# One new order of work for a two-part transformer layer, with w_phi first, Wk ahead, and eight filling products for fourteen

## The chip, the cores and the metric

The kernel runs on one core of one Trainium2 chip. The metric is the time of one execution in microseconds (us), the median of several runs; lower is better. A core has a matrix engine (TensorE, PE in the views, with its weight loads as PEld), VectorE (DVE), ScalarE (ACT), GpSimd (POOL) and SyncE (SP). Each engine works through its own queue strictly in the order of the program; semaphores hold an instruction until what it needs is there. Transfers between memory and the core are issued from the queue of an engine, here SP's or ACT's.

## What is computed

The input has 2048 rows of 640 values, in bfloat16. An attention with feature maps and a gated block follow each other, each behind a layer norm and with its input added:

```python
def _A_ref(x, wqkv, w_phi, wo):          # 32 heads of 20
    q, k, v = ...                        # x @ wqkv, split by head
    pq = einsum("bhsd,hdf->bhsf", q, w_phi)
    pk = einsum("bhsd,hdf->bhsf", k, w_phi)
    phi_q = concat([softmax(pq), softmax(-pq)])
    phi_k = concat([softmax(pk), softmax(-pk)])
    kv = einsum("bhsf,bhsd->bhfd", phi_k, v)
    z  = einsum("bhsf->bhf", phi_k)
    num = einsum("bhqf,bhfd->bhqd", phi_q, kv)
    den = einsum("bhqf,bhf->bhq", phi_q, z)[..., None] + 1e-6
    return (num / den) @ wo

h  = x + _A_ref(layernorm(x), wqkv, w_phi, wo)
n  = layernorm(h)
h2 = h + ((n @ w_gate) * (n @ w_up)) @ w_down
```

## The kernel before

The rows are cut into 16 tiles of 128. The work is a graph of some 1,030 named operations, built in `build_graph`. Each has a name of a kind and a tile. The kinds that the text needs, in the order in which a tile meets them:

- `x0`, `x1`, ... load tiles of x; `w5` loads w_phi; `wk0` to `wk4` and `wv0` to `wv4` load 128 rows each of Wk and Wv; `wqt0` to `wqt4` load Wq transposed. All are transfers.
- `warm0`, ... multiply zeros (lines 367 and 372). They stand in TensorE's queue while it has nothing else; eight come first (L367) and `NFILL` more after (L372).
- `WT0` to `WT4` transpose Wk on TensorE (L392), `WTe0`, ... copy the result out (L251), `Ph0` to `Ph2` spread w_phi into a block matrix Phi on GpSimd (L380), and `F1_0` to `F1_4` multiply Wk by Phi (L411), so that one product gives the argument of the feature map. `Fe1_0`, ... copy that out. `F0_0` to `F0_4` do the same for Wq, and read all five `wqt`.
- `L1s`, `L1a` take the statistics of a tile on VectorE (L428, L429, L431), `L1l`, `L1e` its inverse deviation by a logarithm and an exponential on ScalarE (L436, L439), `L1n` a shift, and `xn` scales the tile (L453 on VectorE, L451 on ScalarE). `xt` transposes the scaled tile: tiles 0 and 1 on TensorE (L462, copied out by `xte`), the others by a transposing transfer from SP's queue (L471).
- `V`, `K`, `Q` are the three projections of a tile (L482); for tiles 0 and 1 each is cut into five pieces (`K0_0` to `K0_4`). `Ve` copies V out (L251). For K, `Kx` are two exponentials (L494), `Ks` their sums (L498), `Kr` and `Ke` a logarithm and an exponential of these (L501, L503), `Kn` the scaling on GpSimd (L518), and `KV` adds the tile to the sum over rows (L526). The Q kinds `Qx`, `Qs`, `Qr`, `Qb`, `Qe`, `Qn` do the like (L551 to L570), and `qT` transposes by a transfer.
- `KVe0` and `KVe1` take the sum out (L533). Then, tile by tile, `N` gives numerator and denominator (L588), `dd`, `rd`, `o` divide, `oT` transposes by a transfer, `O` multiplies by wo (L625), `h` adds x (L631), `hc` and `hT` center and transpose, `L2q`, `L2v`, `L2r` give the second norm's factor.
- The gated block takes the rows in five groups (tiles 0 and 1, 2 to 5, 6 to 9, 10 to 13, 14 and 15, numbered 0 to 4). `U0_1_0` is the product with w_gate for group 0 and columns block 1, `U0_1_1` that with w_up (L668); `g` copies the gate out on ScalarE (L673), `u` multiplies on VectorE (L676). `D` is the product with w_down for a tile (L687), `y` adds (L699) and `w` stores.

What decides the order is the dictionary `PLAN`, read from a long text at the head of the kernel. An entry has the operation's name, a key, the number of an alternative engine and the numbers of the buffer slots, for example:

```python
x1:0.78:1 ekz:0.78 x0:0.78 zero:0.91 id0:1.014 warm0:1.127
```

`arrange` sorts all operations by key, and every engine gets its own in that order. Keys are compared only, so they may be times or ranks. The slots name, among others, the eight banks of PSUM ("psum") in which TensorE leaves its products. An operation that takes a slot waits for the last reader of the one that had it before: so a projection waits for the exponentials or the copy of an earlier one. The waits on semaphores are worked out in `emit` from these orders.

At the head the queues stand as follows before. SP: x0, x3, w5, wk0, wk4, wk1, wk2, x4 (two tiles), wv1, wv0, wv2, wv3, x2, wv4, x6. ACT: x1, wk3. TensorE: 18 products on zeros, WT3, three more, WT0, xt1, WT4, WT1, the last on zeros, F1_0, F1_3, WT2, xt0, F1_1, F1_4, F1_2, then pieces of K0, K1, V1, V0. VectorE: L1s1, L1s0, L1a1, L1s3, L1a0, xn1, L1a3, WTe0, xn0, WTe4, xn3, WTe2, xte0.

Of the kernel before, what the change touches and what calls it, by code (L numbers as in the profile page):

```python
# [69 lines left out]
Fe0_0:26.481 L1s13:26.984 xn9:27.065:1:0 F0_4:27.378::4 K4:27.697::0 Kr5:27.88 Fe0_4:27.895:1 xt9:28.018 Ve6:28.026::6 mk0:28.408 mk1:28.572 Kr2:28.61  # L70
L1s11:28.635 Ke2:28.901 Fe0_2:29.047 KV0:29.053::4,5 Kn2:29.235 wd1:29.328 KV1:29.386 L1s10:29.422 Kx4_0:29.631::2 K7:29.719::2 L1s14:30.209 Kx4_1:30.215
F0_3:31.075::6 L1a14:31.119 L1a10:31.228 Kx7_0:31.275::0 xn8:31.337::1 V7:31.394::0 smz:31.548 Fe0_3:31.859 L1a11:31.867 xt8:31.975 Ks4:31.976::1 Kx7_1:32.443
KV2:32.75 Ke5:33.027 KV3:33.083 L1l10:33.173 wg1:33.285 L1s15:33.369 F0_1:33.416::6 L1e10:33.499 K6:33.735::2 L1n11:33.779 Fe0_1:33.933 Kn5:34.003
# [164 lines left out]
def build_graph():  # L238
# [131 lines left out]
    wm_b = Buf("pwarm", "psum")  # L370
    for k in range(8, 8 + NFILL):
        G.op("pe", "warm%d" % k, lambda e: e.matmul(pb(wm_b)[:, 0:256], lhsT=T["zero"][:, 0:P], rhs=T["zero"][:, :],  # L372
# [556 lines left out]
```

## Time and profile before

| what | value |
|---|---|
| time, median of 3 runs | 271.48 us (271.42 to 271.83) |
| profiled execution, first to last instruction | 270.1 us |
| granted TensorE clock, mean | 1.000 |
| TensorE busy | 264.2 us, 98% |
| VectorE busy | 160.0 us, 59% |
| ScalarE busy | 124.0 us, 46% |
| GpSimd busy | 71.3 us, 26% |

The profile is of one execution. It covers the span from the first to the last instruction; the timed runs hold 1.4 us more, which lie around the span. In a row of the timeline the columns are start, duration from the first start to the last end, engine, line, operation, what is written and read, and the count; in brackets stands the idle time of the engine before it and what ended that. The end of a product is modelled and holds its way through the array, so a run of products is read by its starts. A row of busy time by stretches has, for the stretch, its length, then the busy time of PE, PEld, DVE, ACT and POOL with the number of instructions, the granted clock, the share of the DMA engines and the GB/s. A row of the chain that ended last has start, length and what ran.

### The profile page before, as it was taken

What the parts mean: (1) busy time and instruction counts of PE and PEld (TensorE: products, weight loads), DVE (VectorE), ACT (ScalarE), POOL (GpSimd) and SP (SyncE); (2) the same over time, 40 slices, a digit from 0 to 9 for tenths busy, and PEclk for the clock granted to TensorE, in tenths of its full rate; (3) what the DMA queues carried; (4) which work ended last, traced back from release to release, by engine and by line L of the source; (5) the groups of instructions that cost most, each with busy time, mean ns of one, the idle gap of its engine ahead of it and who ended that gap; (6) DMA issues with size and microseconds to landing.
All of it is one profiled execution on the core that took longest, in us unless ns stands there. A gap on an engine that the chain in (4) does not pass through costs nothing.

```text
span 270.1 us, 5186 instructions
## 1 busy us (share of the span) xinstructions
PE 264.2 (98%) x2092; PEld 177.9 (66%) x2105; DVE 160.0 (59%) x294; ACT 124.0 (46%) x316; POOL 71.3 (26%) x89
## 2 busy tenths in 40 slices
...
GB/s 200 318 168 136 249 222 129 302 183 245 204 106 143 163 126 149 140 123 64 171 93 2 0 0 36 57 106 1 73 12 2 0 0 51 49 1 0 27 49 61
DMA packets 71752, 28.09 MB, mean 104 GB/s; under 512 B 59056, under 2 KB 71728, under 8 KB 71728
## 3 DMA queue, kind: packets, MB, share of 16 engines
...
## 4 chain that ended last, share of the span: by engine, by line
PE 90%; DMA 5%; DVE 2%; ACT 1%; issue 1%; SPq 1%; DVEq 0%
PE ps L668 36%; PE ps L482 24%; PE ps L687 19%; PE ps L625 6%; DMA scratch<-ph 2%; PE ps L526 2%; PE ps L588 2%; DMA Wp<-o 2%; DMA x_all<-in_A_x_dram 1%; PE ps L411 1%; SPq L653 1%; DVE st L428 0%; ACT Wp L251 0%; DVE st L429 0%; DVE ev L676 0%
## 5 line engine op out<-in xcount | busy, mean ns | idle before, releaser
L668 PE MATMUL ps<-xnT,Wgu 128*128 128x512 bf16 (+1 forms) x587 | 106.0, 335 | 0.7
L668 PEld LDWEIGHTS ps<-xnT,Wgu 128*128 128x128 bf16 x600 | 58.3, 98 | 43.4
L673 ACT ACTIVATE gt<-ps 128x512 bf16<-128x512 f32 (+1 forms) x60 | 29.7, 509 | 100.9 <-PE ps L668 62.9
L482 PE MATMUL ps<-Wp,xnT 128*128 128x320 bf16 (+1 forms) x480 | 68.6, 298 | 0.0
L482 PEld LDWEIGHTS ps<-Wp,xnT 128*128 128x128 bf16 x480 | 45.5, 97 | 17.2 <-issue 0.2
L676 DVE TENSOR_TENSOR ev<-ps,gt 128x512 bf16<-128x512 f32 (+1 forms) x60 | 33.6, 579 | 36.5 <-PE ps L668 27.8
L687 PE MATMUL ps<-Wd,ev 128*128 128x320 bf16 (+2 forms) x396 | 53.9, 295 | 0.0
L687 PEld LDWEIGHTS ps<-Wd,ev 128*128 128x128 bf16 x396 | 38.1, 98 | 15.3 <-DVE ev L676 0.2
L699 DVE SCALAR_TENSOR_TENSOR Wp<-ps,rs,x_all 128x640 bf16<-128x640 f32 (+3 forms) x18 | 14.6, 810 | 49.3 <-PE ps L687 49.1
L518 POOL TENSOR_TENSOR ek<-ek,SR 128x1280 bf16<-128x1280 bf16 x16 | 37.5, 2358 | 5.2 <-ACT SR L503 5.1
L551 ACT ACTIVATE ph<-ps 128x600 bf16<-128x600 f32 x32 | 21.4, 680 | 8.0 <-PE ps L482 6.9
L556 DVE TENSOR_REDUCE S<-ph 128x66 f32<-128x1320 bf16 x16 | 23.9, 1516 | 1.8 <-ACT ph L553 1.8
L625 PE MATMUL ps<-Wo,Wp 128*128 128x320 bf16 x160 | 23.9, 299 | 0.2
L498 DVE TENSOR_REDUCE SR<-ek 128x64 f32<-128x1280 bf16 x16 | 23.3, 1468 | 1.0 <-ACT ek L494 1.0
L570 POOL TENSOR_TENSOR ph<-ph,RQ 128x660 bf16<-128x660 bf16 x16 | 20.7, 1308 | 8.9 <-ACT RQ L566 8.9
L646 POOL TENSOR_SCALAR ln<-mv 128x1 f32<-128x1 f32 x12 | 2.3, 191 | 75.7 <-ACT ek L642 75.1
L494 ACT ACTIVATE ek<-ps 128x640 bf16<-128x640 f32 x32 | 21.2, 719 | 2.2 <-PE ps L482 1.5
L625 PEld LDWEIGHTS ps<-Wo,Wp 128*128 128x128 bf16 x160 | 15.3, 98 | 6.4 <-DMA Wp<-o 0.4
L631 DVE SCALAR_TENSOR_TENSOR x_all<-ps,x_all 128x640 bf16<-128x640 f32 x16 | 13.1, 821 | 6.4 <-PE ps L625 6.4
L615 DVE TENSOR_TENSOR o<-ps,sm 128x660 bf16<-128x660 f32 x16 | 13.4, 840 | 0.9 <-ACT sm L608 0.6
L642 ACT ACTIVATE ek<-x_all,mv 128x640 bf16<-128x640 bf16 x16 | 13.1, 821 | 0.0
L251 ACT ACTIVATE ev<-ps 128x640 bf16<-128x640 f32 x16 | 11.2, 704 | 1.1 <-PE ps L482 1.1
...
## 6 DMA issues: line engine op xcount, KB each, us to landing
out_dram<-Wp SPq DMA_DIRECT2D x15, 160.0 KB, 1.8
...
Wp<-in_A_wqkv_dram SPq DMA_DIRECT2D x5, 160.0 KB, 4.7
ev<-in_A_wqkv_dram SPq DMA_DIRECT2D x4, 160.0 KB, 4.2
x_all<-in_A_x_dram SPq DMA_DIRECT2D x3, 160.0 KB, 3.2
```

The source lines that it names most:

```text
L482: ins = e.matmul(pb(b, hb)[:, 0:n1 - n0], lhsT=T["xnT"][:, NC - 1 - c, P * t:P * (t + 1)], rhs=T["Wp"][:, POS[kind], c, n0:n1], start=(c = ...
L494: G.op("act", "%sx%d_%d" % (nm, t, s), lambda e, s=s, b=b, ek=ek: e.activation(out=T["ek"][:, ek.slots[0], 0:2 * D].rearrange("p (b h s f) ...
L498: G.op("dve", "%ss%d" % (nm, t), lambda e, ek=ek, sr=sr: e.tensor_reduce(out=T["SR"][:, sr.slots[0], 0, :], in_=T["ek"][:, ek.slots[0], 0: ...
L518: G.op("pool", "Kn%d" % t, lambda e, eng, ek=ek, sr=sr: e.tensor_tensor(out=T["ek"][:, ek.slots[0], 0:2 * D].rearrange("p (h f) -> p h f", ...
L551: e.activation(out=v[:, 0:10].rearrange("p (b g) j f -> p b g j f", b=2), in_=pp(b, 0, 300).rearrange("p b (g j f) -> p b g j f", j=3, f=D ...
L556: G.op("dve", "Qs%d" % t, lambda e, t=t, ph=ph: e.tensor_reduce(out=T["S"][:, t, 0:66].rearrange("p (g k) -> p g k", k=6), in_=pv(ph).rear ...
L570: return e.tensor_tensor(out=v, in0=v, in1=T["RQ"][:, rq.slots[0], 1, 0:33].rearrange("p (g j) -> p g j", j=3).unsqueeze(3).to_broadcast([ ...
L625: ins = e.matmul(pb(b, hb)[:, 0:320], lhsT=T["oT"][:, oT.slots[0], c, :], rhs=T["Wo"][:, c, 320 * hb:320 * (hb + 1)], start=(c == 0), stop ...
L668: ins = e.matmul(pb(b)[:, 0:n], lhsT=T["Wgu"][:, gu, c, P * ft:P * (ft + 1)], rhs=T["xnT"][:, NC - 1 - c, o0:o0 + n], start=(c == 0), stop ...
L673: G.op("act", "g%d_%d" % (bi, ft), lambda e, pg=pg, gt=gt, n=n: e.activation(out=T["gt"][:, gt.slots[0], 0:n], in_=pb(pg)[:, 0:n], func=AF ...
L676: o_ = G.op("dve", "u%d_%d" % (bi, ft), lambda e, pu=pu, gt=gt, hh=hh, ft=ft, n=n: e.tensor_tensor(out=T["hh"][:, hh.slots[0], ft, 0:n], i ...
L687: ins = e.matmul(pb(b, hb)[:, 0:w], lhsT=T["hh"][:, hh.slots[0], ft, P * tt:P * (tt + 1)], rhs=T["Wd"][:, ft, c0 + w * hb:c0 + w * (hb + 1 ...
```

## The change

`PLAN` is replaced as a whole, with ranks from 0 to 1023 as keys, and `NFILL` goes from 14 to 8. No operation other than six products on zeros is added or dropped, and no formula changes. What moves, by engine:

- SP's queue begins w5, x1, x3, wk0, wk3, wk2, wk1, wv1, wv0, wv2, x2, wv3, x4, x6, wv4, xt3, wqt4, xt2, wqt2, xt4, xt5, wqt3, wqt1, xt6, wqt0. ACT's queue begins x0, wk4, and later issues x8, x10, wu2 and wd3.
- TensorE: 13 products on zeros, WT4, three more, xt0, F1_4, WT0, WT3, xt1, WT2, WT1, F1_0, F1_3, V0_0, V0_1, F1_2, V0_2, F1_1, V0_3, V1_0, K0_0. The projections after these come as K3, V3, K2, V4, K5, V5, V2, V6 (before: K3, V3, K5, V5, K2, V2, V4).
- VectorE begins L1s0, L1a0, L1s1, xn0, L1a1, L1s3, xn1, L1a3, WTe0, WTe3, xte1, WTe1, Fe1_0. Six copies of V (Ve0, Ve1, Ve8, Ve11, Ve13, Ve14) go from ScalarE to VectorE; xn5 and xn6 go to ScalarE, where xn9 was.
- ScalarE from xn2 on: xn2, Kx1_0, L1l4, Kx1_1, L1e4, Kx0_0, Kx0_1, xn5, L1l6, Kx3_0, L1e6, x10, Kx3_1, Kr0, Ve3, xn6, Kx2_0, Kx2_1, Kr1, Ke0, Ke1, Ve4, L1l8, Kx5_0, Kr3, Ve5, L1e8, Ke3, Ve2, Kx5_1.
- The second half has more of group 0 and group 1 before the last numerators, and D5, D4, D3 and D0 behind each other. The last products are D14, D13, D11, D12, D10, D15_1, D15_2 (before: D14, D11, D13, D12, D10, D15_1, D15_2).

The diff, cut to the lines that the text speaks of:

```diff
-NFILL = 14
+NFILL = 8
...
-x1:0.78:1 ekz:0.78 x0:0.78 zero:0.91 id0:1.014 warm0:1.127 id1:1.252 x3:1.26:1 wk3:1.26:1 warm1:1.345 va1:1.496 warm2:1.564 w5:1.74:1 warm3:1.782 warm4:2.001
-warm5:2.219 wk0:2.22:1 eps:2.326 gl0:2.357 warm6:2.437 gla:2.518 warm7:2.656 wk4:2.7:1 glb:2.822 warm8:2.874::0 warm9:3.093 wk1:3.18 warm10:3.311 warm11:3.529
-wk2:3.66:1 L1s1:3.725 warm12:3.748 warm13:3.966 x4:4.14 warm14:4.185 warm15:4.403 L1s0:4.512 wv1:4.62 warm16:4.621 warm17:4.84 wv0:5.1:1 L1a1:5.299 L1s3:5.408
-WT3:5.446::1 L1l1:5.532 wv2:5.58:1 Ph2:5.775 L1e1:5.858 warm18:5.902 warm19:6.011 wv3:6.06 WTe3:6.1:1 warm20:6.12 L1a0:6.195 xn1:6.304::0 Ph1:6.369 x2:6.54
-WT0:6.546::2 L1l0:6.685 Ph0:6.761 L1a3:6.834 xt1:6.971::3 wv4:7.02:1 WTe0:7.023:1 L1l3:7.067 L1e0:7.249 WT4:7.25::4 L1e3:7.393 xte1:7.486 xn0:7.487::1 x6:7.5
-L1n3:7.673 WT1:7.746::5 phz:7.897 WTe4:8.017:1 warm21:8.025 F1_0:8.134::6 WTe1:8.223:1 xn3:8.425::2 F1_3:8.453::0 WT2:8.772::2 Fe1_0:8.808:1 xt0:9.051::3
-xt3:9.063 WTe2:9.249:1 F1_1:9.33::4 Fe1_3:9.392 F1_4:9.649::6 xte0:9.657:1 Fe1_1:9.976 L1s4:10.065 F1_2:10.153::0 x8:10.373 K0_0:10.472::2 Fe1_2:10.67:1
-K0_1:10.743 L1s5:10.852 wqt4:10.853 K1_0:11.014::4 Fe1_4:11.254:1 K1_1:11.285 K1_2:11.556 L1a4:11.639 L1a5:11.762 V1_0:11.827::0 L1l4:11.995 K1_3:12.098
-wqt1:12.163 L1s2:12.225 L1e4:12.321 V0_0:12.369::6 K1_4:12.64 V1_1:12.911 L1n5:13.012:1 Kx1_0:13.11::0 V0_1:13.182 xn5:13.296::3 V0_2:13.453 Kx1_1:13.694
...
-L1l6:18.929 xt4:19.174 L1e6:19.255 Ks3:19.347::1 Ve3:19.348::2 L1n7:19.535 L1n6:19.759 Kx0_0:19.932::2 V5:19.96::0 rqz:19.983 wqt3:20.484 Kx0_1:20.516
...
-L1e8:25.367 F0_0:25.384::0 Kr0:25.46 wg2:25.488 Ks2:25.591::0 L1n8:25.647 F0_2:25.703::6 Ke0:25.751 L1n9:25.871 Ve4:25.897::5 wg0:25.968 V6:26.022::2 Kn0:26.095
...
-N0:74.439::0 Qx6_0:74.637::4 N2:74.772::2 qT4:74.963::2 dd0:74.97::0 Q7:75.105::4 rd0:75.185 Qx6_1:75.247 dd2:75.475::1 o0:75.599::0 rl2:75.857 rd2:76.211
...
-o4:91.048::0 Q15:91.1::2 Qx12_1:91.575 dd7:91.803::2 rd7:92.018 hc9:92.185::3 oT4:92.261::2 o7:92.432::1 U0_1_0:92.719::0 hc2:93.187:1:0 U0_1_1:93.265::1
...
-o14:110.404::2 U1_0_0:110.936::7 L2q3:111.099 u0_7:111.159 hT9:111.572 g0_8:111.939::2 N15:112.015::4 g1_0:112.213::0 U0_10_1:112.348::6 dd15:112.546::1
...
+zero:0 id0:1 x0:2:1 w5:3:1 gl0:4 warm0:5 x1:6 wk4:7 warm1:8 warm2:9 gla:10 x3:11:1 warm3:12 glb:13 warm4:14 eps:15 id1:16 warm5:17 wk0:18:1 warm6:19 warm7:20
+wk3:21 warm8:22::0 warm9:23 wk2:24:1 warm10:25 warm11:26 wk1:27 warm12:28 L1s0:29 Ph2:30 wv1:31 wv0:32:1 Ph0:33 L1a0:34 L1s1:35 WT4:36::7 L1l0:37 wv2:38:1
+warm13:39 L1e0:40 mk0:41 WTe4:42 warm14:43 Sz:44 x2:45 xn0:46::2 Ph1:47 warm15:48 wv3:49 L1a1:50 L1s3:51 va1:52 xt0:53::3 L1l1:54 x4:55 F1_4:56::6 L1e1:57
+WT0:58::1 xn1:59::3 x6:60 Fe1_4:61:1 WT3:62::2 L1a3:63 WTe0:64:1 wv4:65:1 xt1:66::0 L1l3:67 xte0:68 WTe3:69 WT2:70::4 WT1:71::5 xte1:72:1 L1e3:73 F1_0:74::6
+WTe2:75 L1n3:76 WTe1:77 F1_3:78::2 ekz:79 V0_0:80::0 Fe1_0:81 mk1:82 Fe1_3:83 V0_1:84 F1_2:85::4 L1s2:86 V0_2:87 Fe1_2:88:1 F1_1:89::6 V0_3:90 xn3:91::3
+Fe1_1:92 V1_0:93::2 K0_0:94::4 L1a2:95 xt3:96 L1s4:97 V1_1:98 L1l2:99 x8:100:1 K0_1:101 K1_0:102::6 L1s5:103 L1e2:104 K1_1:105 L1n2:106 K1_2:107 wqt4:108
+xn2:109:1:1 K1_3:110 L1a4:111 L1a5:112 K1_4:113 L1s6:114 V1_2:115 Kx1_0:116::4 K0_2:117 K0_3:118 xt2:119 L1s7:120 K0_4:121 L1l4:122 Kx1_1:123 V0_4:124
+V1_3:125 L1a7:126 L1a6:127 L1e4:128 V1_4:129 Kx0_0:130::2 Ve0:131:1:2 wqt2:132 L1n5:133 K3:134::6 L1n4:135 smz:136 Kx0_1:137 phz:138 xn4:139::0 xn5:140:1:2
+Ve1:141:1:1 xt4:142 V3:143::0 L1s9:144 L1l6:145 Kx3_0:146::0 xt5:147 Ks0:148::2 L1e6:149 x10:150:1 K2:151::2 L1n6:152 L1n7:153 Kx3_1:154 wqt3:155 L1s8:156
+Kr0:157 V4:158::6 Ve3:159::0 L1a9:160 xn6:161:1:1 L1a8:162 Ks1:163::1 wqt1:164 K5:165::4 Kx2_0:166::1 Kx2_1:167 Ks3:168::0 xt6:169 Kr1:170 V5:171::0 Ke0:172
+Ke1:173 Ve4:174::3 Kn0:175 wqt0:176 xn7:177::3 L1l8:178 Kx5_0:179::3 V2:180::2 Ks2:181::3 Kr3:182 Ve5:183::4 xt7:184 L1e8:185 Ke3:186 V6:187::6 L1s10:188
+L1n8:189 Ve2:190::5 L1n9:191 Kn1:192 wo2:193 Kx5_1:194 L1a10:195 L1s11:196 x14:197 F0_4:198::2 Kr2:199 Ke2:200 F0_2:201::0 xn9:202::2 Fe0_4:203 K4:204::4
...
+Ks14:420::2 Qn2:421 V11:422::0 Ke12:423 Kn12:424 qT2:425::3 Kr14:426 Qr4:427::2 Q13:428::6 Ke14:429 Ve11:430:1:0 Ve12:431::1 Qb9:432:1 Qs10:433 V13:434::0
...
+KV15:450 Qb10:451 qT9:452::1 Qb4:453:1 Q6:454::6 Qr13:455::3 Qe4:456 KVe0:457 Qb13:458 Qn4:459 KVe1:460 Qx6_0:461::3 N0:462::4 N2:463::2 qT4:464::2 dd0:465::3
...
+N5:512::4 hT0:513 h1:514 O3:515::0 Qr7:516::2 Qe10:517 hc2:518:1:3 Qn10:519 Qb7:520:1 dd5:521::1 Qe7:522 hc1:523::0 Q14:524::2 h3:525 rl5:526 Qn7:527 hT1:528
+rd4:529 rd5:530 o5:531::0 O9:532::0 o4:533::1 Qx14_0:534::2 oT5:535::3 Qx14_1:536 Q12:537::4 Qs6:538 qT10:539::0 N13:540::2 h9:541 Qr6:542::3 U0_1_0:543::6
...
+U0_5_1:599::2 g0_6:600::1 hT4:601 U0_8_0:602::1 Qr8:603::1 u0_5:604 Qb8:605 U0_9_1:606::7 u0_6:607 Qb11:608 g0_8:609::3 g0_7:610::0 U0_10_0:611::5 qT6:612::2
...
+U1_1_1:627::3 L2q1:628 dd10:629::3 u0_9:630 rd10:631 L2q2:632 o10:633::0 U1_0_1:634::2 rd7:635 u0_10:636 Q15:637::0 L2r0:638 o7:639::2 L2v1:640:1 hc9:641:1:3
...
+U1_10_0:727::3 qT12:728::0 O14:729::0 U1_7_0:730::7 qT11:731::3 h14:732 u1_5:733 U1_7_1:734::4 g1_7:735::1 u1_6:736 g1_10:737::0 N15:738::0 g1_8:739::3
...
+hT7:768 O15:769::4 dd12:770::3 L2r4:771 hT6:772 D5_0:773::0 h15:774 hc15:775::1 L2q13:776 D4_0:777::4 y5_0:778::2 rd12:779 o12:780::2 L2r3:781 hc14:782:1:2
...
+y14_0:1005::0 D11_0:1006::6 y13_0:1007::2 w13_0:1008 w14_0:1009 D12_0:1010::0 y11_0:1011::1 D10_0:1012::3 y12_0:1013::2 w12_0:1014 w11_0:1015 D15_1:1016::5
...
```

More of the change, by code (lines that the diff above doesn't have):

```diff
@@ L70 @@
[L70 to L73, printed above, removed]
@@ new lines @@
+Qx5_0:282::1 L1a14:283 L1a12:284 L1a13:285 Qs1:286 Kr6:287 Q3:288::4 Ke6:289 Qx5_1:290 Kn6:291 L1l12:292 Ks9:293::3 Qr1:294::0 Ve7:295::2 K10:296::0 Ke7:297
+L1e12:298 Qx3_0:299::2 L1n15:300:1 xn15:301::0 L1n13:302 KV4:303 Qb1:304 KV5:305 Kn7:306 xn13:307::3 xt15:308 Kx10_0:309::2 KV6:310 Qs0:311 K8:312::6
+Kx10_1:313 Qx3_1:314 xt13:315 Ks10:316::0 Kr9:317 K11:318::0 Ke9:319 Qe1:320 Kx8_0:321::1 Kn9:322 wg1:323 Kx8_1:324 L1n12:325:1 V8:326::4 Kx11_0:327::3
+Ks8:328::1 Kx11_1:329 Q9:330::6 Kr10:331 L1n14:332 Qn1:333 Ve8:334:1:5 Kr8:335 Qr0:336::1 wu2:337:1 xn12:338::3 KV7:339 Ke8:340 Qb0:341 Qx9_0:342::4
```

119 lines of the change are left out of this document (45 added, 74 removed).

## The prediction

> **What bounds the kernel now.** I read the page first, then busy time by stretches, then the head's timeline, then the chain that ended last.
>
> ```profile
> PE 264.2 (98%) x2092; PEld 177.9 (66%) x2105; DVE 160.0 (59%) x294; ACT 124.0 (46%) x316; POOL 71.3 (26%) x89
> 20.00:30.00 10.00, 10.00 (x104) 7.64 (x103) 8.29 (x13) 9.87 (x24) 6.32 (x9) 1.00 0.81 177
> 84.00:94.00 10.00, 9.76 (x90) 7.09 (x89) 9.31 (x20) 4.90 (x15) 2.81 (x3) 1.00 0.81 143
> 104.00:114.00 10.00, 9.51 (x98) 7.23 (x98) 6.25 (x16) 5.49 (x17) 2.23 (x4) 1.00 0.89 131
> 113.00 0.51 PE L588 MATMUL ps<-KVm,scratch 128*128 128x63 bf16 x11 [0.44 <-DMA scratch<-ph]
> 249.64 18.05 PE ps L687 x144
> 267.78 0.32 DVE Wp L699
> ```
>
> TensorE is busy 98% of the span. From 20 to 30 us it has no gap at all, with ScalarE at 9.87 of 10 us beside it; in two later stretches 0.24 and 0.49 us are missing, 0.44 of them one wait of numerator product N15 for its transpose. The chain ends in 18 us of L687 and one small eviction. So only three things can move the time: the head, gaps that the new order opens or closes, and the tail. The tail keeps its order: both plans end D12, D10, D15_1, D15_2, so I cost it at nothing.
>
> ```profile
> 0.83 0.40 ACTq L285 DMA_DIRECT2D x_all<-in_A_x_dram  x1
> 1.72 0.43 SPq L285 DMA_DIRECT2D w<-in_A_w_phi_dram  x1
> 2.19 1.95 SPq L285 DMA_DIRECT2D ev<-in_A_wqkv_dram  x4
> 2.80 2.34 PE L372 MATMUL ps<-ev 128*128 128x256 bf16 x10
> 3.91 0.49 DVE L428 BATCH_NORM_STATS2 st<-x_all 128x6 f32<-128x320 bf16 x1 [2.85 <-DMA x_all<-in_A_x_dram]
> 4.72 0.48 DVE L428 BATCH_NORM_STATS2 st<-x_all 128x6 f32<-128x320 bf16 x1
> 4.85 0.43 PEld L392 LDWEIGHTS ps<-ident,ev 128*128 128x128 bf16 x5 [0.20 <-DMA ev<-in_A_wqkv_dram]
> 5.30 0.49 PE L372 MATMUL ps<-ev 128*128 128x256 bf16 x3
> 5.50 0.19 DVE L431 BATCH_NORM_AGGREGATE mv<-st 128x2 f32<-128x12 f32 x1
> 6.13 1.68 POOL L380 TENSOR_TENSOR Phi<-w,GL 128x280 bf16<-128x280 bf16 x3 [2.47 <-DMA w<-in_A_w_phi_dram]
> 6.47 0.55 DVE L453 TENSOR_SCALAR xn<-x_all,mv,rs 128x640 bf16<-128x640 bf16 x1
> 6.49 0.45 PE L392 MATMUL ps<-ident,ev 128*128 128x128 bf16 x5 [0.70 <-DMA ev<-in_A_wqkv_dram]
> 7.37 0.72 PE L392 MATMUL ps<-ident,ev 128*128 128x128 bf16 x10
> 8.04 0.80 PE L411 MATMUL ps<-Phi,scratch 128*128 128x140 bf16 x12
> 9.15 0.49 DVE L251 COPY scratch<-ps 128x640 bf16<-128x640 bf16 x1
> 10.22 0.48 PE L411 MATMUL ps<-Phi,scratch 128*128 128x140 bf16 x6 [0.19 <-ACT Wp L251]
> 10.54 5.73 PE L482 MATMUL ps<-Wp,xnT 128*128 128x320 bf16 x41
> 27.65 0.32 PE ps L411 x6
> ```
>
> Before, the folds (L411) begin at 8.04, right behind Phi (6.13 + 1.68 = 7.81), and w_phi, third on SP's queue, landed only at 6.13. After the last fold, projections run unbroken from 10.54. I use 10.54 as the start of the stretch that TensorE bounds.
>
> **The change: the head.** One fold costs 0.32. In the new order all seven transposes and F1_4 stand ahead of F1_0, F1_3, F1_2, F1_1, and four pieces of V0 stand between these. The comparable moment before, with four folds left, is 10.54 - 4 x 0.32 = 9.26.
>
> When is it after? x0 now leaves from ACT's queue as x1 did (0.83, used at 3.91), so DVE starts at 3.9. A pair of statistics takes 0.81 (3.91 to 4.72), and from an aggregate to the scaling that follows took 6.47 - 5.50 = 0.97. So L1s0 ends 4.7, L1s1 5.6, xn0 6.2, L1s3 7.0, xn1 7.55. x of tile 3 is third on SP, where w_phi landed at 6.13, in time for L1s3. w_phi leaves first; by x1's 3.1 us it lands at 3.9, and Phi's 1.68 us plus two short memsets end near 6.2. F1_4 follows tile 0's transpose at about 6.5, so Phi no longer gates.
>
> ```profile
> L285 SPq DMA_DIRECT2D ev<-in_A_wqkv_dram x4: 432/432/523, 2.2 to 3.7; - x4
> DMA to landing us min/median/max: 3.6/4.1/4.3
> ```
>
> Wk is late next. Four blocks still leave SP between 2.2 and 3.7, so the last, wk1, lands at 3.7 + 4.1 to 4.3, about 7.9. TensorE transposes tile 1 from 7.6, then WT2 and WT1 (two took 0.72 with the drain, 0.28 each in steps), and F1_0 starts at 8.5. Its inputs are ready: DVE copies WT0 out by 8.15 and WT3 by 8.6 (0.49 or less each). Gain 9.26 - 8.5 = 0.75; I take **0.65**, bounds 0.2 (x1 delayed behind w_phi's packets) and 0.9.
>
> The six products fewer on zeros cost nothing directly. The cover that goes with them is a rival below.
>
> **ScalarE from 13.7 to 27.** Fold products for Q and the next projections need PSUM banks that ScalarE empties.
>
> ```profile
> 15.39 0.91 ACT L451 ACTIVATE xn<-x_all,nb,rs 128x640 bf16<-128x640 bf16 x1
> 16.48 0.44 ACTq L285 DMA_DIRECT2D x_all<-in_A_x_dram  x1
> 18.44 0.71 ACT L251 ACTIVATE ev<-ps 128x640 bf16<-128x640 f32 x1
> 20.06 2.48 ACT L494 ACTIVATE ek<-ps 128x640 bf16<-128x640 f32 x4
> 22.39 0.29 ACT L501 ACTIVATE SR<-SR 128x64 f32<-128x64 f32 x1
> 25.49 0.80 PE L411 MATMUL ps<-Phi,scratch 128*128 128x140 bf16 x12
> 26.29 1.36 PE ps L482 x10
> ```
>
> Four exponentials in 2.48 give a step of 0.59. From Kx1_0 to Kx5_1 the new queue holds 10 exponentials and 4 evictions of V (14 x 0.59 = 8.3), xn5 and xn6 (2 x 0.81 in steps, 1.6), six short logarithms (0.3 each, 1.8), six short exponentials (0.14 each, 0.8), a wait of about 0.3 for Ks0, and the issue of x10 (0 to 0.44: the row before stands beside a wait, so it does not show whether it blocks). Sum 12.8 to 13.2. xn2 stands ahead of Kx1_0 here and lets it start near 13.7, so Kx5_1 ends at 26.5 to 26.9. Without gaps TensorE wants that bank for K4 at 26.8: from F1_0 stand 4 folds, 11 projections of 1.36 (V0, V1, K0, K1, K3, V3, K2, V4, K5, V5, V2), V6 and two Q folds, 8.5 + 1.3 + 16.3 + 0.6 = 26.7. So 0 to 0.3 is lost there, and a like tightness stands at V4 (behind Kx3_1, about 19.4) and K10 (behind Qx5_1). I take **+0.3**, bounds 0 and 0.9. Six evictions of V move from ScalarE to DVE; they load it with some 6 x 0.7 = 4 us, but DVE's 8.29 of 10 in that stretch has room, and Ve14 and Ve11 still end before V12 and V13 need their banks.
>
> **SP's queue.** The last transpose of Wq stands behind six of x.
>
> ```profile
> L309 SPq DMA_TRANSPOSE scratch<-in_A_wqkv_dram x5: 1167/1271/2227, 11.1 to 21.2; - x5
> DMA to landing us min/median/max: 3.2/4.2/5.0
> ```
>
> Before, the last was issued at 21.2 and the first Q fold ran at 25.49. Now wqt0 comes behind xt6, which waits for xn6 on ScalarE (about 21.4 by the count above). With 1.27 an issue it leaves at 23.3 and lands at 26.5 to 28.3. F0_4, whose bank Ve2 empties near 26.4, needs it then. The low end is likelier, since the neighbours are small then: **+0.1**, bounds 0 and 1.8. Those bounds are a rival below. The other moves on SP (weights of the second half) leave tens of us to their use.
>
> **After KV15.**
>
> ```profile
> 74.74 0.84 PE L588 MATMUL ps<-KVm,scratch 128*128 128x63 bf16 x22
> 101.75 0.55 PE ps L668 x5
> 128.49 1.08 PE ps L668 x5
> ```
>
> Between Q15 and N15 stood 19 narrow groups of gate and up products (0.55) and 2 wide ones (1.08), 12.6 us; now it is 2 and 17, 19.5 us, so N15's wait of 0.44 for its transpose goes. What is late next: the transpose hT1 ahead of U0_1_0, behind L2q0 and two short steps on ScalarE, hT4 ahead of U1_1_1, oT15 ahead of O15. Counted through their queues in the same way they have, by estimate, 0.7 to 0.9 to spare. I take **-0.15**, bounds -0.6 and +0.7.
>
> **Sum.** -0.65 + 0.3 + 0.1 - 0.15 = -0.4. The span of 270.1 becomes 269.7; the median of the runs, 271.48, lies 1.4 above the span, so the time is **271.1**. About 0.2%, 0.54 us, is what a measurement of this kernel tells from no change.
>
> **Rivals.**
>
> *Everything fits (270.3).* The head gives 0.75, ScalarE's queue keeps ahead, and both late gaps close (0.24 + 0.49 less a little): 271.48 - 0.75 - 0.45 = 270.3. For it: ScalarE gets rid of six evictions. Against: three margins under 0.3 all have to hold.
>
> *The clock (272.0).* Ten zero products took 2.34, so with the last one's 0.42 a step of 0.21; three from 5.30 took 0.49, a step of 0.11.
>
> ```profile
> L372 PE MATMUL ps<-ev x14: 272/421/421, 2.8 to 7.9; 128*128 128x256 bf16 x14
> ```
>
> TensorE went at half speed until about 5.1, four us after its first product at 1.12. Now thirteen products end near 4.1 and the queue stands until Wk's first block lands at 4.85. If that gap restarts the count, full speed comes at 4.85 + 4.0 = 8.85. The work from 6.1 to 8.5 (seven blocks of about 0.3, 2.1 us) would take 2.75 for its first 1.4 and end at 9.5 in place of 8.5: 1.0 later, some of it in slack, 0.9 net: 272.0. Against: TensorE still works four fifths of those four us (13 x 0.21 and the start of the transposes), and nothing shows what share is needed.
>
> The Trainium skill (TensorE: Matmul & The Clock Gate, "What's actually happening") says that the clock opens after about 3.4 us of sustained work, in a window that runs free of the kernel's start. By that rule the gap spoils the window that ended at 5.1, and the time is this rival's. The trace before agrees with the rule as far as it goes: half speed for four us, then full; no run here shows a head with a gap yet.
>
> *Wq late (272.9, slower).* wqt0 takes 5.0 us to land, as the slowest did, since x10 of two tiles leaves from ACT some 4 us ahead of it. F0_4 then starts at 28.3, 1.8 late, and everything behind it on TensorE's queue shifts: 271.1 + 1.8 = 272.9. It decides from a landing time of 3.2 on; the median of 4.2 costs 0.9. For it: two of the three slowest shared the queues with loads of x. Against: the last two, issued in quiet, took the least.
>
> **Chances.** Forecast 0.38 (faster 0.12, same 0.22, slower 0.04). Everything fits 0.20, all faster. Clock 0.22 (same 0.10, slower 0.12). Wq late, or another late transpose of like price, 0.20, all slower. That gives faster 0.32, same 0.32, slower 0.36. The range from 270.3 to 273.0 leaves out 0.1 on each side.
>
> **What would show it.** Right: the first fold of the last four at 8.5, K4 near 27, the first numerator product near 74.4 where it was 74.74, no wait of L588 for scratch. Clock: zero products and the first transposes at 0.21 and 0.11 a step beyond 6 us. Wq: an idle TensorE ahead of L411 near 26, released by the DMA into scratch. Wrong altogether: gaps over 0.5 us after 74, or x of tile 1 landing past 5.5.

## The result, and the profile after

| kernel | median us | runs | against before, same chip |
|---|---|---|---|
| before | 271.83 | 271.42 to 272.19 (5) | 1 |
| after | 275.23 | 272.94 to 276.18 (5) | 1.0122, 95% interval 1.0086 to 1.0158 |

The change costs 3.4 us; 271.1 was forecast, with a range up to 273.0. The profiled execution of after took 275.41 us, its span 273.6. All its lines stand 22 lower than in before (L482 is L460, L471 is L449).

First the page's row of busy time, then the stretches, then the end of the chain, all of after, as they were shown of before:

```profile
PE 265.8 (97%) x2083; PEld 179.3 (66%) x2099; DVE 162.9 (60%) x302; ACT 123.5 (45%) x315; POOL 69.8 (26%) x82
```

```profile
20.00:30.00 10.00, 8.73 (x67) 6.12 (x66) 8.96 (x15) 7.75 (x19) 4.62 (x6) 1.00 0.74 155
84.00:94.00 10.00, 9.75 (x90) 7.10 (x88) 9.04 (x20) 5.32 (x16) 3.88 (x3) 1.00 0.82 125
104.00:114.00 10.00, 9.94 (x97) 7.96 (x97) 6.59 (x17) 5.75 (x17) 4.31 (x6) 1.00 0.63 96
```

```profile
253.23 17.46 PE ps L665 x132
...
271.30 0.32 DVE Wp L677
```

The stretch from 20 to 30 us, which had no gap, now lacks 1.27 us of TensorE. The one from 104 to 114 us, which lacked 0.49, is nearly full, and the tail is what it was. So the loss lies early. These stretches are cut by time and hold somewhat different work in the two kernels; a count by products says the same. By the starts of weight loads N0 comes 4.5 us later than before (79.10 against 74.60), and from N0 to D10_0 after takes 186.9 us against 187.8.

The timeline of after between 12 and 24 us shows where most of it goes:

```profile
12.85 1.87 SPq L449 DMA_TRANSPOSE xnT<-xn  x1
12.98 0.40 ACTq L263 DMA_DIRECT2D x_all<-in_A_x_dram  x1
...
17.51 3.92 PEld L460 LDWEIGHTS ps<-Wp,xnT 128*128 128x128 bf16 x30 [0.78 <-DMA xnT<-xn]
...
18.72 2.60 SPq L449 DMA_TRANSPOSE xnT<-xn  x2
19.09 0.40 ACTq L263 DMA_DIRECT2D x_all<-in_A_x_dram  x1
...
23.03 6.63 PEld L460 LDWEIGHTS ps<-Wp,xnT 128*128 128x128 bf16 x50 [1.60 <-DMA xnT<-xn]
```

K3 (17.51) waits 0.78 us for the transposing transfer xt3, and V4 (23.03) 1.60 us for xt4. In both cases ScalarE issues a load of two tiles of x right behind the transpose (x8 at 12.98, x10 at 19.09, that is 0.13 and 0.37 us later), and that load lands first. The answer by source line for after's transposes of x gives their way from issue to landing; xt2, issued at 16.1 between the two, has none issued within 2.9 us of it:

```profile
L449 SPq DMA_TRANSPOSE xnT<-xn x1: 1870/1870/1870, 12.8 to 12.8; - x1
DMA to landing us min/median/max: 4.6/4.6/4.6
...
L449 SPq DMA_TRANSPOSE xnT<-xn x1: 1276/1276/1276, 18.7 to 18.7; - x1
DMA to landing us min/median/max: 4.3/4.3/4.3
...
L449 SPq DMA_TRANSPOSE xnT<-xn x1: 1275/1275/1275, 16.1 to 16.1; - x1
DMA to landing us min/median/max: 2.9/2.9/2.9
```

In before, xt3 is slow too: it left at 9.14, with loads in flight ahead of it, and took 5.5 us to land, but it left 3.7 us earlier, and nobody waited.

The second loss stands in after's timeline from 70 to 80 us:

```profile
70.93 4.67 POOL L496 TENSOR_TENSOR ek<-ek,SR 128x1280 bf16<-128x1280 bf16 x2
71.66 1.68 DVE L541 TENSOR_TENSOR RQ<-RQ 128x32 f32<-128x32 f32 x1
73.26 1.51 DVE L534 TENSOR_REDUCE S<-ph 128x66 f32<-128x1320 bf16 x1
74.81 0.26 ACT L537 ACTIVATE RQ<-S 128x64 f32<-128x64 f32 x1 [2.88 <-DVE S L534]
76.36 0.73 ACT L229 ACTIVATE ev<-ps 128x640 bf16<-128x640 f32 x1
77.14 0.40 PEld L504 LDWEIGHTS ps<-ev,ek 128*128 128x128 bf16 x11 [0.84 <-ACT ev L229]
79.10 0.75 PEld L566 LDWEIGHTS ps<-KVm,scratch 128*128 128x128 bf16 x22 [0.41 <-issue]
```

Read upward from KV15 (77.14): it waits 0.84 us for Ve15, which stands in ScalarE's queue behind Qr10, which waits 2.88 us for VectorE's sum Qs10, which stands behind Qb9. That is a subtraction of 32 numbers a row, and it takes 1.68 us, up to 0.05 us behind the end of GpSimd's product Kn12 (73.29). N0 waits 0.41 us more; 0.32 to 0.33 of this stays where KV15 does not wait (e6, e7), so that part is not Qb9's.

### The profile page after: what moved, and what is told of

Same layout as the page of the kernel before. It is cut to its first block, busy times and chain, and to the rows that moved or that the text cites. A ratio compares the mean times of both kernels' runs of the same rounds, so it can differ in the third digit from the quotient of the medians.

```text
span 273.6 us, 5164 instructions
## 1 busy us (share of the span) xinstructions
PE 265.8 (97%) x2083; PEld 179.3 (66%) x2099; DVE 162.9 (60%) x302; ACT 123.5 (45%) x315; POOL 69.8 (26%) x82
## 4 chain that ended last, share of the span: by engine, by line
PE 90%; DMA 4%; DVE 3%; ACT 2%; issue 1%; POOL 0%; DVEq 0%
PE ps L646 38%; PE ps L460 21%; PE ps L665 19%; PE ps L603 6%; PE ps L566 2%; DMA xnT<-xn 2%; PE ps L504 2%; PE ps L389 1%; DMA x_all<-in_A_x_dram 1%; DMA Wp<-o 1%; PE ps L370 1%; DVE x_all L609 1%; DVE S L534 1%; ACT ek L472 0%; PE ps L440 0%
## 5 line engine op out<-in xcount | busy, mean ns | idle before, releaser
L651 ACT ACTIVATE gt<-ps 128x512 bf16<-128x512 f32 (+1 forms) x60 | 29.1, 509 | 96.8 <-PE ps L646 82.3
L460 PE MATMUL ps<-Wp,xnT 128*128 128x320 bf16 (+1 forms) x480 | 69.1, 299 | 1.7 <-DMA xnT<-xn 1.7
L460 PEld LDWEIGHTS ps<-Wp,xnT 128*128 128x128 bf16 x480 | 45.5, 97 | 20.0 <-DMA xnT<-xn 2.4
L665 PEld LDWEIGHTS ps<-Wd,ev 128*128 128x128 bf16 x396 | 38.2, 98 | 15.1
L624 POOL TENSOR_SCALAR ln<-mv 128x1 f32<-128x1 f32 x7 | 1.3, 192 | 72.6 <-ACT ek L620 72.4
L618 ACT ACTIVATE xn<-x_all,mv 128x640 bf16<-128x640 bf16 x10 | 8.0, 821 | 7.9 <-DVE x_all L609 5.2
```

Source lines behind the costliest of these rows:

```text
L460: ins = e.matmul(pb(b, hb)[:, 0:n1 - n0], lhsT=T["xnT"][:, NC - 1 - c, P * t:P * (t + 1)], rhs=T["Wp"][:, POS[kind], c, n0:n1], start=(c = ...
L651: G.op("act", "g%d_%d" % (bi, ft), lambda e, pg=pg, gt=gt, n=n: e.activation(out=T["gt"][:, gt.slots[0], 0:n], in_=pb(pg)[:, 0:n], func=AF ...
L665: ins = e.matmul(pb(b, hb)[:, 0:w], lhsT=T["hh"][:, hh.slots[0], ft, P * tt:P * (tt + 1)], rhs=T["Wd"][:, ft, c0 + w * hb:c0 + w * (hb + 1 ...
```

## The experiments

Theory after reading the two traces: TensorE waits for transposing transfers that plain loads hold, and for a VectorE instruction that GpSimd holds. Rivals: the clock, a queue on SyncE that is too long anyway, and the second half's new order.

In the table, idle time of TensorE's weight loads ahead of a product, in us, in the profiled execution (under 0.1 left out). The column "x" is the projection of tile 4, 5 or 6 that waits for its transpose. F1_0 is given where the head is the new one. e8 and e12 have a joined order, before's up to N0 and after's behind it. All times are medians of the runs, the waits are of one execution; e2 and e11 are in the text.

| kernel | F1_0 at | K3 | x | F0_4 | KV15 and N0 | N9 | O9 and U0_0_1 | median |
|---|---|---|---|---|---|---|---|---|
| after | 9.74 | 0.78 | 1.60 | | 1.25 | | | 275.23 |
| e15 (after again) | 8.43 | 0.67 | 1.37 | | 1.25 | | | 275.04 |
| e1 | 8.32 | 1.01 | 2.40 | | 1.25 | | 1.02 | 275.59 |
| e3 | 8.67 | 0.94 | 1.91 | | 1.25 | | 1.01 | 275.60 |
| e4 | 8.38 | 0.82 | 1.32 | | 1.24 | | | 275.12 |
| e5 | 8.23 | 0.66 | | 0.68 | 1.25 | | | 274.27 |
| e6 | 9.62 | 0.85 | 1.80 | | 0.33 | 0.86 | 1.02 | 275.03 |
| e13 | 9.79 | 0.83 | 0.88 | | 1.25 | | | 274.55 |
| e9 | 8.29 | 1.45 | 0.90 | 0.34 | 0.33 | 0.51 | | 274.29 |
| e10 | 8.30 | | 0.44 | 0.78 | 0.32 | 0.74 | 0.95 | 273.63 |
| e7 | 8.25 | 1.02 | 0.25 | 0.83 | 0.32 | 0.72 | | 273.15 |
| e14 | 8.27 | 1.20 | | 0.34 | 0.32 | 0.77 | | 272.63 |
| e8 (joined order) | | | | | | | 0.97 | 270.99 |
| e12 (joined order) | | | | | | | | 270.82 |

The table leaves out Q10 and V12 (0.27 to 0.29 and 0.18 to 0.19 in all twelve with the new head), V0_3, which waits for wv3 (1.48 in e15, 0.61 in e5), K2 in e10 (0.69), and waits of O0, O2 or O3 between N0 and O9, the longest 1.17 for O0's transpose in e1 and e3. The diffs below show the changed entries of `PLAN` alone, not their whole lines.

**The clock, the zero products and x10 (e1 to e4).** First the rival of the clock. e1 is after with six products on zeros put into the gaps that stood at 4.1 and 5.4 us:

```diff
-NFILL = 8
+NFILL = 14
+warm16:28.1 warm17:28.2 warm18:28.3 warm19:48.1 warm20:48.2 warm21:48.3
```

> The new order with fourteen filling products again: three more behind the thirteenth, so that TensorE works on until Wk's first block is there, and three more behind the sixteenth. Clock theory (TensorE stays at half speed until 10.6 us because its products stop at 4.1, and the late transposes follow from that): full speed at about 5.1, F1_0 near 8.2 where it stood at 9.74, K3 near 15.5 in place of 17.5, time 271 to 272, and the runs lie within 1 us of each other. Rival, the loads and transposes of the new order (xt4 landed 4.3 us after its issue beside x10): the head gains its 1.3 us at most, V4 still waits for xt4, time 273.5 or more.

Measured: 275.59 us (274.16 to 276.50), ratio 1.0127 (1.0099 to 1.0156). F1_0 comes at 8.32, 1.4 us earlier, and V4's wait grows from 1.60 to 2.40. Half of the gain is waited away at the transposes: N0 still comes 0.8 us earlier than in after (78.33). The rest goes behind N0, where O0 waits 1.17 for its transpose and O9 and U0_0_1 1.02. e2 is before with eight such products (warm16 to warm21 go):

```diff
-NFILL = 14
+NFILL = 8
-warm13:3.966 warm14:4.185 warm15:4.403
+warm13:5.902 warm14:6.011 warm15:6.12
...
```

> The kernel before with eight filling products in place of fourteen and nothing else: thirteen products on zeros ahead of WT3, three behind it, so that TensorE's work stops near 4.1 until Wk's block lands at 4.85. Clock theory: full speed comes later than 7 us in most runs, the first projection later than 11.5 where it stood at 10.5, time 272.5 to 274.5 with a spread of 1 us or more. Rival (the order, not the filling, costs the time): 271.5 to 272.1 as before.

Measured: 272.38 us, ratio 1.0020 (0.9998 to 1.0041). That lies between the two forecasts. In before's order the count of these products explains at most 0.4%, of a loss of 1.2%. e3 is after with x10 behind wqt3 on SyncE's queue:

```diff
-x10:150:1
+x10:155.5
```

> The new order, with the load of x of tiles 10 and 11 moved from ScalarE's queue to SP's, behind wqt3, so that it no longer runs beside xt4. Transposes theory: xt4 lands 2.8 us after its issue in place of 4.3, V4 starts 1.3 us earlier, time 1 to 1.5 lower than the new order's. Clock theory: xt4 lands earlier, but its lateness is only a part of the loss; 0.3 to 1.3 lower, and the spread of the runs stays.

Measured: 275.60 us, ratio 1.0117 (1.0081 to 1.0152). V4 comes 2.7 us earlier (20.32; 1.1 us of it since F1_0 comes earlier in this execution), its wait falls to 0.20, and V6 waits 1.71 in its place. e4 joins e1 and e3:

> Both edits: fourteen filling products and the load of tiles 10 and 11 behind wqt3 on SP. Clock theory: within 0.5 us of the kernel with the filling products alone. Transposes theory: at least 1 us below it. If both hold and nothing else is left, the time is 270.5 to 271.3, below the kernel before.

Measured: 275.12 us, ratio 1.0100 (1.0071 to 1.0129). So neither the clock nor x10 alone carries the loss, nor both together, and KV15's wait is the same in after, e1, e3 and e4.

**The two waits, and the two halves (e5 to e8).** e5 loads both x8 and x10 ahead of the transposes; e6 moves Qb9 to GpSimd; e7 does both.

```diff
-x8:100:1 x10:150:1
+x8:65.5 x10:65.6
```

```diff
-Qb9:432:1
+Qb9:432
```

> After, with the loads of x8 and x10 (two tiles of x each) issued by SyncE directly behind w_v's part 4, so that both have landed before the first transposing DMA. In the profile of after the product K3 waits 0.78 us and V4 waits 1.60 us, each for a transposing DMA (xt3 and xt4) whose landing came 1.1 us and 0.2 us behind that of one of these loads, 4.6 and 4.3 us after its issue where undisturbed ones take 2.6 to 2.9 us. Theory 1 (a transposing DMA is held by a load that is in flight): xt3 and xt4 land 2.6 to 3.2 us after their issue, both waits are under 0.3 us, and the time falls by their sum less what F0_4 gives back to the last transpose of W_q: 1 to 2 us, to 273.2 to 274.2 us. Rival (the queue itself is the limit, as when only x10 was moved: a later transposing DMA is late by as much): the waits move to V6 and F0_4, and the time stays at 275 us.

Measured: 274.27 us (272.92 to 276.48), ratio 1.0087 (1.0051 to 1.0122). xt4 lands 2.7 us after its issue, and the wait for it is gone. K3's stays, since x10 now lands at 15.45 and xt3 0.6 us behind it; F0_4 takes back 0.68 for wqt0. Theory 1 holds for the transfer without a load beside it; the forecast for K3 fails, and the saving of 1.0 us falls just short of the range. The interval overlaps that of after.

> After, with one subtraction (Qb9, 128 rows by 32 numbers) moved from VectorE to GpSimd and nothing else. In the profile of after it takes 1.68 us on VectorE (others of its kind 0.18 us there and 0.24 us on GpSimd), from 71.66 to 73.34 us, and GpSimd's product Kn12 ends at 73.29 us. Theory 2 (VectorE is held in this operation until GpSimd's instruction is over; behind it the sum Qs10, the logarithm Qr10 and, on ScalarE's queue, the copy Ve15 come late, for which KV15 waits 0.84 us, and N0 0.41 us behind it): both waits go, N0 starts about 1 us earlier against V15, and the time falls by 0.5 to 1.2 us, to 274.0 to 274.7 us. Rival (Ve15 is late because ScalarE has two exponentials ahead of it anyway): the wait of KV15 stays above 0.5 us, and the time at 275.2 us.

Measured: 275.03 us, ratio 1.0108 (1.0079 to 1.0138). KV15's wait is gone and N0's down to 0.33, as theory 2 says. The time does not follow: N9 waits 0.86 us for its transpose qT9 and O9 0.76 for h3. A wait taken away alone was worth 0.2 us, which is within the noise. N9 waits in every kernel with Qb9 on GpSimd (0.51 to 0.86); O9's wait comes from Qb7, as shown below.

> After with both edits: x8 and x10 loaded ahead of the transposing DMAs, and Qb9 on GpSimd. If both theories hold the savings add, 1.5 to 3.2 us together: 272.0 to 273.7 us, which would leave under 2 us of the loss of 3.4 us. If either saving only moves a wait: 274 us or more. If what is lost lies somewhere else (the clock, the new order's own pace): 275 us.

Measured: 273.15 us (272.18 to 274.36), ratio 1.0047 (1.0026 to 1.0067): 2.1 us of the 3.4, and the interval lies clear of after's. The medians of the two alone fell by 1.0 and 0.2, neither clear of after's, so how the 2.1 us divide between the two is not shown.

e8 takes before's order up to N0 and after's for all that is left, with that part's slots assigned anew:

```diff
+Qr10:462::0 KV15:463 Q6:464::6 KVe0:465 Qb13:466 KVe1:467 N0:468::0 Qb10:469 Qx6_0:470::4 N2:471::2 qT4:472::2 dd0:473::0 Qx6_1:474 Q7:475::4
...
```

Up to `N0:468` this is before's order, from `Qb10:469` on after's.

> The order of before up to and with the product N0, then the order of after for all that is left (PSUM and SBUF slots of that part assigned anew). From N0 to D10_0 after took 186.9 us in its profile and before 187.8 us. Theory 3 (all of the loss lies ahead of N0, and the new order is faster behind it): 270.6 to 271.3 us, N0 at 74.6 us as in before and D10_0 187 us behind it. Rival (the order behind N0 is only as fast as it was because more had been done ahead of it by then): 272 us or more, with new waits between N0 and U0_1_0.

Measured: 270.99 us (270.60 to 272.26), ratio 0.9966 (0.9949 to 0.9983). In its profile N0 comes at 74.38 and D10_0 187.5 us behind it. Theory 3 holds: all of the loss lies ahead of N0, and behind before's first half the new order of the second is the faster one, by 0.3%.

**SyncE's queue (e9, e10).** e9 has Qb9 on GpSimd and two transposes of Wq in the idle time of SyncE's queue ahead of xt3:

```diff
-wqt4:108 wqt2:132 wqt3:155 wqt1:164 wqt0:176 x8:100:1 x10:150:1
+wqt4:65.5 wqt1:65.6 wqt2:96.5 x8:119.5 wqt3:119.6 x10:147.5 wqt0:147.6
```

> After with Qb9 on GpSimd and SyncE's queue set anew between 8 and 24 us: behind w_v's part 4 the order is wqt4, wqt1, xt3, wqt2, xt2, x8, wqt3, xt4, xt5, x10, wqt0, xt6, xt7 (two transposes of W_q go into the 3 us in which SyncE waits for xn3, the loads of x8 and x10 stand behind xt2 and xt5, and wqt0 leaves some 3 us earlier). When x8 and x10 were loaded ahead of xt3, K3 still waited 0.66 and 1.02 us (xt3 landed 0.6 us behind x10) and F0_4 0.67 and 0.83 us (for wqt0). Theory 4 (what is left of the loss is this queue): both waits go, N0 comes 66.2 us or less behind F1_0 (67.5 us with both edits before this one, 69.4 us in after), and the time is 271.4 to 272.4 us. Rival (behind the queue ScalarE's copies and exponentials are the limit of the new order there, up to 0.9 us of wait for F0_4's slots): 272.6 to 273.2 us, with F0_4 or K4 waiting for ScalarE.

Measured: 274.29 us, ratio 1.0083 (1.0057 to 1.0109), 1.1 us worse than e7. Theory 4 fails. F0_4, for which wqt0 is in by 24.6, waits 0.34 us for its bank, which ScalarE's copy Ve2 leaves at 28.01: that is the rival's wait, but the time lies above the rival's too. The answer by source line for the wqt4 of this kernel:

```profile
L287 SPq DMA_TRANSPOSE scratch<-in_A_wqkv_dram x1: 1222/1222/1222, 8.2 to 8.2; - x1
DMA to landing us min/median/max: 6.9/6.9/6.9
```

The loads of x6 and wv4 ahead of it were in at 12.95, and it landed at 15.1; wqt1 and xt3 followed 0.6 us apart, and K3 waited 1.45. e10 is e7 (from which its diff is taken) with xn3 earlier on VectorE and the loads behind xt3:

```diff
-xn3:91::3 x8:65.5 x10:65.6
+xn3:85.5::3 x8:96.5 x10:96.6
```

> After with Qb9 on GpSimd, x8 and x10 loaded by SyncE directly behind xt3 in place of ahead of it, and the normalized tile xn3 ahead of the statistics L1s2 on VectorE, so that xt3 leaves some 0.7 us earlier and with nothing in front of it but the loads up to w_v's part 4, which land near 13 us. With the loads ahead of xt3 it landed 4.6 us after its issue at 15.81 us and K3 waited 1.02 us. Theory 1 (a load in front of a transposing DMA holds it): xt3 lands by 15.1 us, K3 waits under 0.4 us, N0 comes 66.9 us or less behind F1_0 (67.5 us before), and the time is 272.2 to 272.8 us against 273.15 us. Rival (the wait moves behind F0_4, which waits for wqt0 in any case until 27.4 us): K3 comes earlier, F0_4 does not, and the time stays at 273.0 to 273.4 us.

Measured: 273.63 us, ratio 1.0080 (1.0050 to 1.0110). xt3 lands at 15.21, ahead of the two loads issued 1.4 and 2.0 us behind it, and K3 does not wait, but K2 and V4 wait 0.69 and 0.44, and F0_4 starts at 27.66 (27.49 in e7). It went as the rival has it, a little above its time: in e5, e7 and e10 F0_4 starts at 27.5 to 27.7, straight behind the landing of wqt0 (27.4 to 27.6), the last of ten transposes at 1.27 us an issue. The forecast had F0_4 at 26.1.

**Two starts 0.1 us apart (e11 to e15).** The joined order's timeline around 86 us (VectorE, GpSimd, TensorE; its lines stand 4 higher than after's):

```profile
86.04 1.30 POOL L552 TENSOR_TENSOR ph<-ph,RQ 128x660 bf16<-128x660 bf16 x1 [5.30 <-ACT RQ L548]
86.16 1.24 DVE L545 TENSOR_TENSOR RQ<-RQ 128x32 f32<-128x32 f32 x1
...
87.42 0.81 DVE L613 SCALAR_TENSOR_TENSOR x_all<-ps,x_all 128x640 bf16<-128x640 f32 x1
...
88.38 0.84 PE L607 MATMUL ps<-Wo,Wp 128*128 128x320 bf16 x5 [0.41 <-DVE x_all L613]
```

Qb7 starts 0.12 us behind GpSimd's Qn10 and ends 0.05 us behind it; h3 comes late, and O9 waits. In after's profile the same two start the other way round:

```profile
91.16 0.18 DVE L541 TENSOR_TENSOR RQ<-RQ 128x32 f32<-128x32 f32 x1
91.22 2.58 POOL L548 TENSOR_TENSOR ph<-ph,RQ 128x660 bf16<-128x660 bf16 x2 [5.81 <-ACT RQ L544]
```

Ahead by 0.06 us, Qb7 takes 0.18. e11 moves it to GpSimd behind Qn10, in the joined order; e12 puts it there ahead of Qn10:

```diff
-Qb7:528:1
+Qb7:528
```

```diff
-Qb7:528:1
+Qb7:526.5
```

> The joined order (before up to N0, after behind it; 270.99 us) with the one subtraction Qb7 moved from VectorE to GpSimd. In the joined order's profile Qb7 takes 1.24 us on VectorE, from 86.16 us, beside GpSimd's product Qn10 (86.04, 1.30 us); the sum h3 starts behind it at 87.42 us, and O9 waits 0.71 us for h3. Theory 2 (VectorE is held until GpSimd's instruction is over): Qb7 takes 0.24 us on GpSimd, h3 starts 1.1 us earlier, the wait of O9 goes, and the time falls by 0.3 to 0.7 us, to 270.3 to 270.7 us. Rival (what is saved on VectorE turns into a wait for Qb7's own readers or for the next sum): 271.0 us, with Q12 or U0_0_1 waiting longer than 0.12 and 0.26 us.

Measured: 271.98 us, ratio 1.0004 (0.9989 to 1.0020), 1.0 us worse than e8. The wait went where the rival has it, and the time above the rival's 271.0. Timeline of e11, GpSimd, ScalarE, TensorE:

```profile
88.50 0.24 POOL L545 TENSOR_TENSOR RQ<-RQ 128x32 f32<-128x32 f32 x1
88.77 0.23 ACT L548 ACTIVATE RQ<-RQ 128x32 f32<-128x32 f32 x1 [1.61 <-POOL RQ L545]
...
91.03 1.54 PE L464 MATMUL ps<-Wp,xnT 128*128 128x300 bf16 x10 [0.68 <-DVE o L597]
```

Behind Qn10 it ends at 88.74, ScalarE's queue stands 1.61 us for it, VectorE's division waits for ScalarE, and Q12 for the bank that the division reads, in place of O9.

> The joined order with Qb7 on GpSimd ahead of Qn10 (in e11 it stood behind it, and its reader on ScalarE came late). Theory 5 (VectorE is held there in most executions of the joined order): Qb7 takes 0.24 us at about 86 us, h3 starts near 86.4 us in place of 87.42 us, O9 and U0_0_1 do not wait, and the time falls from 270.99 us to 270.0 to 270.5 us. Rival (the wait goes to Q12 again, as with Qb7 behind Qn10): 271 us or more.

Measured: 270.82 us (270.61 to 271.16), ratio 0.9959 (0.9946 to 0.9971): the lowest median of the study. Timeline of e12:

```profile
86.44 0.24 POOL L545 TENSOR_TENSOR RQ<-RQ 128x32 f32<-128x32 f32 x1 [5.56 <-ACT RQ L541]
86.64 2.57 POOL L552 TENSOR_TENSOR ph<-ph,RQ 128x660 bf16<-128x660 bf16 x2
...
86.98 0.82 DVE L613 SCALAR_TENSOR_TENSOR x_all<-ps,x_all 128x640 bf16<-128x640 f32 x1 [0.30 <-PE ps L607]
```

O9 and U0_0_1 do not wait. The median fell by 0.2 us, less than expected and inside the two intervals; the longest run fell from 272.26 to 271.16.

e13 is after with that one edit (`Qb7:520:1` to `Qb7:517.5`), e14 is e7 with it, e15 is after unedited.

> After with the same one edit alone: Qb7 on GpSimd ahead of Qn10. Theory 5: 0.7 to 1.1 us less than after in most executions, a median of 274.1 to 274.6 us. Rival (in after the subtraction comes first in most executions, as in its profile): 275.0 to 275.4 us.

Measured: 274.55 us (274.31 to 274.83), ratio 1.0098 (1.0078 to 1.0119).

> After with x8 and x10 loaded behind w_v's part 4, Qb9 on GpSimd, and Qb7 on GpSimd ahead of Qn10. Theory 5: 272.0 to 272.5 us against 273.15 us without the last edit, which would leave at most 0.6 us of the 3.4 us unaccounted for. Rival: 273 us.

Measured: 272.63 us (272.01 to 274.97), ratio 1.0043 (1.0021 to 1.0065).

> The changed kernel itself once more, on the same chip as the three edits. Theory 5: if Qb7 takes about 1.28 us in this profile, N0 to U0_1_0 is 17.7 us or more and the execution is not among the shortest of its kernel; if it takes 0.18 us, the stretch is 16.8 to 17.2 us. The time: 275 us as before.

Measured: 275.04 us (273.57 to 276.29), ratio 1.0118 (1.0084 to 1.0151). In its profile (274.83 us) Qb7 came first, and N0 to U0_1_0 took 16.83 us. So the medians fall by 0.5 us in each of after and e7, and e14 misses its range by 0.1; the intervals overlap, so that the edit is worth this is not shown. The six runs of e13 spread over 0.5 us, those of e15 over 2.7; but e14's still spread over 3.0, so this is not the whole of the spread. Of the ten profiles of after's order with Qb7 on VectorE, six had it first (N0 to U0_1_0 in 16.8 to 17.2 us) and four second (e1, e3, e6, e10: 17.5 to 18.0). That it is held in most executions, as theory 5 says, the profiles do not bear out.

e15 shows one more thing. The same kernel waits elsewhere in another execution. TensorE's timeline of e15:

```profile
12.03 4.79 PE L460 MATMUL ps<-Wp,xnT 128*128 128x320 bf16 x34 [1.29 <-DMA Wp<-in_A_wqkv_dram]
...
23.81 1.40 PE L460 MATMUL ps<-Wp,xnT 128*128 128x320 bf16 x9 [1.04 <-DMA xnT<-xn]
```

Here V0_3 waits for wv3, V4 does not wait, and x10 catches xt5 in place of xt4 (K5, 23.81): xt4 left 0.92 us ahead of x10 and landed after 2.7 us, xt5 0.36 us behind it and took 4.7. In e13 it went the same way (2.9 and 4.1 us).

## Why the prediction was wrong, step by step

**The head: mechanism right, gain lost.** F1_0 was put at 8.5. In the twelve profiles with the new head it comes at 8.2 to 8.7 nine times. But K3 behind it needs xt3, which leaves behind xn3, and xn3 stands behind Fe1_0 and L1s2 on VectorE: issued at 12.85 where before had 9.1. The prediction lets TensorE run without gaps from F1_0 on, and had no row for that.

**The clock: the sign came, the price was small.** The signs named were zero products at 0.21 and transposes at 0.11 a step beyond 6 us. After's profile has them, its repeat has not. TensorE's timeline of after, then that of e15:

```profile
4.94 0.85 PE L350 MATMUL ps<-ev 128*128 128x256 bf16 x3
7.18 1.27 PE L370 MATMUL ps<-ident,ev 128*128 128x128 bf16 x10
9.85 1.15 PE L389 MATMUL ps<-Phi,scratch 128*128 128x140 bf16 x12
```

```profile
6.78 0.72 PE L370 MATMUL ps<-ident,ev 128*128 128x128 bf16 x10
...
8.49 0.80 PE L389 MATMUL ps<-Phi,scratch 128*128 128x140 bf16 x12
```

Ten transposes take 1.27 us against 0.72, and F1_0 is 1.3 us later. That fell on three of ten profiles with eight zero products in the new head (after, e6, e13) and on neither of the two with fourteen. The Trainium skill's page "TensorE: Matmul & The Clock Gate" ("What's actually happening") describes a window that runs free of the kernel's start, by which the opening varies by about 0.5 us either way. That two executions of one kernel differ fits it; but they open at 3.8 and 10.6 us, far more than that, so the page alone does not account for it. The clock is not the cause of the 3.4 us: e1 has full speed early and the same median, and e15's execution, early too, took 274.83 us against after's 275.41.

**SyncE's queue: the step that failed.** It was sized +0.1, up to 1.8, for wqt0 alone. The rival "Wq late" named the mechanism, x10 from ScalarE's queue in front of a transpose, and put F0_4 at 28.3; it came at 29.70. But it took the wrong transposes: x8 and x10 hold xt3, and xt4 or xt5, for which projections wait at once. K3 and V4 lose 2.38 us. The other transposes of x were moved past loads too, and the prediction costed none of them: "another late transpose of like price" has a share of a chance and no row. It read the landing times of Wq's transposes alone, though before's trace had slow ones of x as well (xt3 5.5 us to land, xt5 3.9, 0.74 us behind x10).

**ScalarE, +0.3: hardly seen.** K4 was not late for its bank in any profile; it runs straight behind the Q folds, which come too late for ScalarE to matter. A wait for ScalarE at F0_4 shows in e9 alone, 0.34 us. What the prediction said of V12 and the late exponentials missed by a little: V12 waits 0.18 to 0.19 us for Ve14, which went to VectorE, and Q10 0.27 to 0.29 for ScalarE's exponentials.

**KV15: between two terms.** The sum had a term up to F0_4 and one "after KV15". KV15's own wait and N0's, 1.25 us, lay between. Qb9 stood on VectorE in before too, at 56.65, where it took 0.18 us; the diff puts it straight ahead of Qs10 and beside Kn12 (`Qb9:55.781:1` to `Qb9:432:1`). The price of that place was in before's trace, where Qb4 on VectorE takes 2.21 us beside Kn12 with nobody waiting; the prediction read neither. Of the 1.25, about 0.92 is Qb9's; 0.33 stays at N0 with Qb9 on GpSimd.

**After N0: right, and too small.** N15's wait went, as argued. N0 to D10_0 gained 0.9 us in the two profiles (-0.15 was taken, -0.6 the bound). In that profile of after Qb7 came first; where it comes second, about 0.9 us goes again, by the means of the ten profiles up to U0_1_0.

The steps add up: 269.7 was forecast for the span. With 1.2 at F1_0, 2.4 at K3 and V4, 1.25 at KV15 and N0, 0.5 at Q10 and V12 (0.29 and 0.19), less 0.75 behind N0 and less the 0.4 of two terms that did not come, it is 273.9; measured 273.6. The 1.2 belongs to that execution: with e15's waits (1.48 at V0_3 in place of it, 2.04 at K3 and K5) the same sum gives about 273.7, measured 273.1.

Still open: e14 is 0.8 us above before, with waits of 1.20, 0.34, 0.32 and 0.77 us left at K3, F0_4, N0 and N9, and smaller ones of 0.30 and 0.23 at K9 and O3. e9 and e10 only moved those of them that hang on SyncE's queue. How much of e7's 2.1 us each of its two edits gives is not shown either. What makes the clock open late in one execution and not in the next wasn't tried.
